# A change of banks that waits on TensorE's own semaphore instead of a drain, with a softmax round lent into the wait, and a loop that begins earlier

## The chip, the cores and the metric

One core of one Trainium2 chip. The metric is device time in microseconds of one execution. Engines are called as the profile calls them: PE (TensorE's matmuls), PEld (its weight loads), DVE (VectorE), ACT (ScalarE), POOL (GpSimd), SP (SyncE, which issues most transfers).

## The reference, cut to what matters

```python
def reference(A_x, A_wqkv, A_wo, B_x, B_w1, B_b1, B_w2, B_b2, gate_w):
    x = A_x                                   # 1 x 2048 x 576, float32
    g = sigmoid((x * gate_w).sum(-1, keepdims=True))
    a = attention(x, A_wqkv, A_wo)            # 32 heads of 18, full softmax, then @ wo
    b = gelu(layernorm(x) @ B_w1 + B_b1) @ B_w2 + B_b2     # 576 -> 4608 -> 576
    return g * a + (1 - g) * b
```

## The kernel before

Float32 operands are split into a high and a low part of TensorE's faster float32 format, and a product is the sum of three (high by high, high by low, low by high). The kernel has three stages.

The first makes q, k and v of all heads and the normalised input of the network, and stores them. The last multiplies the attention's output with wo and writes the result. Between them lies a loop of 512 steps that does the attention, and into it the network (the "mixer" of the reference) is cut in pieces. There is no scheduler: each engine runs its instructions in the order in which the Python code issues them (`tc.manual_schedule()`), and waits on semaphores for the other engines. So the order of the code is the order on TensorE.

The attention works in 32 units (a pair of heads by half of the queries), 16 steps each. What it issues:

- a *round* (`s1_round`, lines L202 and L204): two matmuls of 54 rows that make scores in two PSUM buffers, one for each head, and two maxima over them on VectorE. A unit has 32 rounds, and they run about 40 rounds ahead of the unit's exponentials, since those need each row's maximum. The PSUM pool `ps_s1` has three buffers (`NS1 = 3`), so a matmul of a round needs the buffer of the third matmul before it, and with it that one's maximum. `next_round()` issues the next round of a list of 1024.
- *scores* (`s2`, L251 and L253): two matmuls of 56 rows into one PSUM buffer (`pss`, there is one), and one exponential of 128x1024 on ScalarE that frees it.
- *values* (`pv`, L268), every other step: the probabilities of two steps by v.

The network is a Python generator (`mlp`) that yields after each *slot*, a pair of matmuls that work side by side in the array's upper and lower 64 rows. `h_pair` is an *up pair*: 27 slots of 64x512 (L489) that make two hidden tiles in two PSUM buffers, their eviction with the bias (L511 on VectorE, L512 on ScalarE), and then the gelu on ScalarE and GpSimd over the next steps. `out_pair` is an *output pair*: 24 slots of 64x288 (L614) that make 128 tokens by 576 outputs, in two PSUM banks, one for each half of the outputs. In its first 12 slots the upper rows write bank 0 and the lower rows bank 1; then they change places, so that each bank gets the sums of both. Both must not write one bank at once. So the change of banks has a wait:

```python
                elif turn == 1:
                    nc.tensor.drain()
```

(L603; 137 of the 144 output pairs. The last 7, after the last round, take other buffers instead.) At the pair's end VectorE adds both banks to the result (L593). The network is 36 groups of two up pairs and four output pairs.

`atom()` runs the generator to its next cut, and `fill(step, share)` puts one such piece at one of three places of two steps, share 0, 1 or 2. An output pair that begins in share 0 is cut after slots 7 and 15: it gets 7, 8 and 9 slots, and the change of banks, behind slot 12, lies in the piece of share 1. Two steps read so (r a round, s scores, v values): step even: r s v s r, 7 slots; step odd: r s, 8 slots with the drain behind the fifth, r s, 9 slots.

Ahead of the loop 36 rounds are done, and between the last of them pieces of up pairs stand (`between(n)`: n pieces of some 600 ns of work, each followed by `run_due`, which issues what is due on the other engines). In the loop's first steps each even step has one more round (`if step <= 2 * LEAD`, LEAD is 4).

Of the kernel before, what the change touches and what calls it, by code (L numbers as in the profile page):

```python
# [10 lines left out]
AF = mybir.ActivationFunctionType  # L11
ALU = mybir.AluOpType
# [16 lines left out]
G = 4  # L29
NFC = F // P  # L30
NG = NFC // G
ND = 288
# [7 lines left out]
LEAD = 4  # L40
# [18 lines left out]
def gated_mix_kernel(ctx: ExitStack, tc: tile.TileContext, x, wqkv, wo, w1, b1, w2, b2, gate_w, out):  # L59
    nc = tc.nc  # L60
# [101 lines left out]
    NU = 2 * NPAIR  # L162
    UNITS = [divmod(u, 2) for u in range(NU)]
    UNITS[NU - 3:NU - 1] = UNITS[NU - 2], UNITS[NU - 3]
    NR = 32
# [146 lines left out]
                defer(1, lambda: s1_finish(u))  # L312


    def mlp():
        W1, W2, HT = {}, {}, {}
        RAW = {}
# [147 lines left out]
        def h_pair(q, last, inner=False):  # L465
# [8 lines left out]
            ps = banks(q)  # L474
# [34 lines left out]
            zs = [ring2[:, 0, k, :] if q == 1 else zp.tile([P, TB], F32, name="z") for k in range(2)]  # L509
            b = [b1t[:, fc + h:fc + h + 1] for h in range(2)]  # L510
            nc.vector.tensor_scalar(zs[1], ps[1], b[1], None, op0=ALU.add)  # L511
            nc.scalar.activation(zs[0], ps[0], AF.Identity, bias=b[0])  # L512
            for h in (1, 0):
                z = zs[h]
                w = ring2[:, 1, h, :] if q == 1 else zp.tile([P, TB], F32, name="zz", bufs=3)
# [67 lines left out]
        def out_pair(i, t, acc):  # L583

            tb, g = seq[i]
            tok = slice(t * P, (t + 1) * P)
            cs = [slice(nn * ND, (nn + 1) * ND) for nn in range(2)]
            bare = not rounds

            def add(ps, base):  # L590
                for nn in range(2):
                    dst = acc[:, t, cs[nn]]
                    nc.vector.scalar_tensor_tensor(dst, ps[nn][:, :ND], 0.5, b2b[:, cs[nn]] if base else dst,  # L593
                                                   op0=ALU.mult, op1=ALU.add)
            ps = [psum(free_pool()) for _ in range(2)]
            ends = {7, 15} if piece[0] == 0 else cuts(24, (3, 2, 1)[piece[0]])
            k = 0
            for turn in range(2):
                if turn == 1 and bare:
                    add(ps, g == 0)  # L600
                    ps = [psum(free_pool()) for _ in range(2)]
                elif turn == 1:
                    nc.tensor.drain()  # L603
                for j in ORDER:
                    while (i, j) not in HT:
                        cut[0] = 3
                        yield 0
                    hh, hl = HT[i, j]
                    w_ = ready(W2, (i * (G // 2) + j // 2, j % 2))
                    for h_, p_ in ((hh, 0), (hh, 1), (hl, 0)):  # L610
                        for h in (0, 1) if turn == 0 else (1, 0):
                            r = slice(64 * h, 64 * h + 64)
                            nn = h ^ turn
                            nc.tensor.matmul(ps[nn][:, :ND], h_[r, tok], w_[p_][r, cs[nn]],  # L614
                                             start=(k == 0 or bare and k == 3 * G), stop=(k == 6 * G - 1 or bare and k == 3 * G - 1))
                        k += 1
                        if k < 6 * G:
                            if k in ends:
                                cut[0] = 1
                            yield 131  # L620
            add(ps, g == 0 and not bare)
            if g == NG - 1:
                tt = TBS[tb] * 4 + t
                nc.gpsimd.tensor_scalar(acc[:, t, :], acc[:, t, :], gate1[:, tt:tt + 1], 1.0, op0=ALU.mult, op1=ALU.mult)
                defer(12 if tb < NB - 1 else 4, lambda: nc.sync.dma_start(b_scr[tt * P:(tt + 1) * P, :], acc[:, t, :]))
            cut[0] = 2
            yield 131
# [407 lines left out]
    RING.append(ring2)  # L1035


    def out_proj():

        OT, BT, done, tmp = {}, {}, {}, {}  # L1040
# [162 lines left out]
    def between(n):  # L1203
        for part in range(n):
            t = spent[0]
            stretch(600.0)
            run_due(max(spent[0] - t, 500.0))

    while len(rounds) > NU * NR - NR - LEAD:
        between(6 if len(rounds) == NU * NR - NR else 2)  # L1210
        next_round()
        run_due(233.0)
    between(1)
    base = spent[0]
    proj = out_proj()
    over = [None]
# [29 lines left out]
    for u in range(NU):  # L1246
        for kc in range(NT):
            step = u * NT + kc
            if kc == 1:
                if u + 2 < NU:  # L1250
                    load_q(u + 2)
                if u % 2 == 0 and u // 2 + 1 < NPAIR - 1:
                    load_k(u // 2 + 1)
                    load_v(u // 2 + 1)
                elif u == NU - 5:
                    load_k(NPAIR - 1)
                elif u == NU - 4:
                    load_v(NPAIR - 1)
            at[0] = step

            next_round()
            s2(u, kc, 0)
            run_due(462.0)
            if kc % 2:
                fill(step, 1)
            elif step > 0:
                pv(step - 2)
                while ROWS:
                    ROWS.pop(0)()
                run_due(2080.0)  # L1270
                if step <= 2 * LEAD:
                    next_round()
            else:
                fill(step, 2)
            if kc % 2:
                next_round()
            s2(u, kc, 1)
            if kc % 2 == 0:

                next_round()  # L1280
            run_due(462.0)
            fill(step, 2 if kc % 2 else 0)
    pv(NSTEP - 2)
# [28 lines left out]
```

## Time and profile before

| | |
|---|---|
| median of 3 runs | 2326.66 us (2324.75 to 2327.2) |
| the profiled execution | 2327.55 us, span 2325.8 us |
| PE busy | 2295.2 us, 99% |
| DVE, ACT, POOL busy | 72%, 59%, 41% |
| drains at L603 | 137 |
| first exponential of the loop | 253.2 us from the span's start |
| last round | 2192.8 us |

Matmuls are pipelined and their ends are modelled, so a PE that is 99% busy can still be slower than it could be: what counts is the distance between the starts of matmuls. "idle before" is the engine's idle time in front of an instruction, and what stands behind the arrow is what ended it. DRAIN and waits are the sequencer's, and not counted as busy.

### The profile page before, as it was taken

Reading aid. Unit: us, or ns where it says so; the run is one execution under the profiler, and the core shown is the slowest. Engines: PE = TensorE matmul, PEld = TensorE weight load, DVE = VectorE, ACT = ScalarE, POOL = GpSimd, SP = SyncE. Lnnn points to the kernel's source line nnn. Section 1 sums busy time; section 2 is a strip of 40 time slices with the busy share of each in tenths; the row PEclk is TensorE's granted clock in tenths of the full one; section 3 lists DMA queues with packets and bytes.
Section 4 is the critical chain, followed back from the end, with each engine's and each line's share of the span. In section 5 each row is a group of like instructions: output and inputs, shape, how many; then the busy total and the mean of one; then the engine's idle time right before and its main releaser. Section 6 shows DMA issues by size and latency. Waiting matters only on the chain.

```text
span 2325.8 us, 50689 instructions
## 1 busy us (share of the span) xinstructions
PE 2295.2 (99%) x20601; PEld 1615.4 (69%) x20601; DVE 1663.7 (72%) x2921; ACT 1379.9 (59%) x1631; POOL 947.8 (41%) x936
## 2 busy tenths in 40 slices
PE   8999999999999999999999999999999999999999
PEld 7878666666666666666666666666666666666669
DVE  5675777777777777777777777777777777777545
ACT  4223666666666666666666666666666666666662
POOL 4002466566553434443444344434434443333320
PEclk9999899999999999999999999999999999999999
DMA  7756545445473524232263324233364233322346
GB/s 242 247 190 197 175 144 170 157 136 169 139 187 131 164 86 127 96 118 96 90 174 144 114 94 134 81 118 116 118 162 153 94 118 107 106 97 101 113 139 223
DMA packets 160654, 323.58 MB, mean 139 GB/s; under 512 B 56062, under 2 KB 83618, under 8 KB 149586
## 3 DMA queue, kind: packets, MB, share of 16 engines
q1 hardware_dynamic: 156582, 313.57, 43.1%
q10 hardware_dynamic: 3840, 6.78, 0.8%
q8 instruction: 162, 2.65, 0.5%
q14 instruction: 70, 0.57, 0.1%
HBM read 229.07 MB, written 95.16 MB: 139 GB/s over the span
## 4 chain that ended last, share of the span: by engine, by line
PE 90%; POOL 3%; DVE 2%; issue 2%; DMA 1%; ACT 1%; SPq 0%; ACTq 0%; POOLq 0%; DVEq 0%
PE ps L614 20%; PE ps L268 19%; PE ps L489 17%; PE pss L251 12%; PE ps L202 11%; PE ps L880 4%; PE ps L1184 3%; PE ps L898 2%; POOL zz L159 1%; POOL w L159 1%; POOL hl L159 1%; DVE m L204 1%; DMA wraw<-in_B_w_dram 1%; PE ps L795 0%; DMA p<-in_A_wqkv_dram 0%
## 5 line engine op out<-in xcount | busy, mean ns | idle before, releaser
L204 DVE TENSOR_REDUCE m<-ps 128x1 f32<-128x512 f32 x2048 | 1297.3, 684 | 431.2 <-PE ps L202 429.7
L253 ACT ACTIVATE p<-pss 128x1024 f32<-128x1024 f32 x684 | 701.7, 1026 | 456.9 <-PE pss L251 445.3
L489 PE MATMUL ps<-big,w 64*128 64x512 f32 x3834 | 514.8, 392 | 0.1
L614 PE MATMUL ps<-w,hh 64*128 64x288 f32 x4352 | 501.2, 300 | 13.8 <-ACT z L512 2.1
L159 POOL TENSOR_SCALAR zz<-zz 128x512 f32<-128x512 f32 x272 | 169.3, 622 | 827.4 <-ACT zz L575 761.8
L251 PE MATMUL pss<-qa,ka 56*128 56x512 f32 x2048 | 484.1, 437 | 3.8 <-ACT p L253 1.1
L253 ACT ACTIVATE ring<-pss 128x1024 f32<-128x1024 f32 x340 | 348.9, 1026 | 231.4 <-PE pss L251 225.6
L202 PE MATMUL ps<-ka,qa 54*128 54x512 f32 x2048 | 460.8, 410 | 2.8 <-DVE m L204 1.2
L614 PEld LDWEIGHTS ps<-w,hh 64*128 64x128 f32 x4352 | 402.4, 186 | 68.9 <-issue 42.4
L489 PEld LDWEIGHTS ps<-big,w 64*128 64x128 f32 x3834 | 390.1, 185 | 59.6 <-ACT vt L909 0.3
L159 POOL TENSOR_TENSOR zz<-zz,z 128x512 f32<-128x512 f32 x280 | 361.4, 1291 | 35.6 <-ACT zz L577 10.5
L251 PEld LDWEIGHTS pss<-qa,ka 56*128 56x128 f32 x2048 | 198.0, 185 | 254.6 <-ACT p L253 121.4
L614 PE MATMUL ps<-w,hl 64*128 64x288 f32 x2176 | 351.7, 293 | 0.0
L268 PE MATMUL ps<-p,vt 128*32 128x512 f32 x2736 | 344.5, 598 | 0.0
L202 PEld LDWEIGHTS ps<-ka,qa 54*128 54x128 f32 x2048 | 244.5, 185 | 34.0 <-DVE m L204 12.1
L614 PEld LDWEIGHTS ps<-w,hl 64*128 64x128 f32 x2176 | 236.2, 186 | 0.5
L159 POOL TENSOR_TENSOR w<-x,w 128x576 fp32r<-128x576 f32 (+1 forms) x34 | 68.3, 2012 | 308.8 <-ACT w L385 304.6
L159 POOL TENSOR_TENSOR hl<-zz,hh 128x512 fp32r<-128x512 f32 x134 | 174.1, 1300 | 19.0 <-ACT hh L538 8.1
L268 PE MATMUL ps<-ring,vt 128*32 128x512 f32 x1360 | 179.1, 598 | 0.0
L268 PEld LDWEIGHTS ps<-p,vt 128*32 128x32 f32 x2736 | 71.4, 109 | 147.3 <-issue 147.3
L593 DVE SCALAR_TENSOR_TENSOR x<-ps,x 128x288 f32<-128x288 f32 x270 | 110.8, 452 | 29.8 <-PE ps L614 16.4
L880 PE MATMUL ps<-big,wqk 128*128 128x512 f32 x504 | 123.4, 399 | 0.1
(122 smaller groups left out, 1403.3 us busy)
## 6 DMA issues: line engine op xcount, KB each, us to landing
w<-w_scr SPq DMA_DIRECT2D x54, 1152.0 KB
w<-w_scr SPq DMA_DIRECT2D x108, 576.0 KB
w_scr<-w SPq DMA_DIRECT2D x18, 1152.0 KB
w_scr<-w SPq DMA_DIRECT2D x36, 576.0 KB
qa<-qk_scr SPq DMA_DIRECT2D x192, 72.0 KB
ka<-qk_scr SPq DMA_DIRECT2D x90, 144.0 KB
x<-in_B_w_dram SPq DMA_DIRECT2D x34, 288.0 KB
qk_scr<-hh SPq DMA_DIRECT2D x36, 256.0 KB
```

The costliest lines, as they stand in the source:

```text
L159: fn(*args, **kw)
L202: nc.tensor.matmul(ps, qa[r0:r0 + 54, t * P:(t + 1) * P], ka[r0:r0 + 54, kb * TB:(kb + 1) * TB], start=True, stop=True)
L204: nc.vector.tensor_reduce(M4[u][:, h, t, kb:kb + 1], ps, axis=AX.X, op=ALU.max)
L251: nc.tensor.matmul(ps[:, h, :], ka[r0:r0 + 56, kc * P:(kc + 1) * P], qa[r0:r0 + 56, qb * TB:(qb + 1) * TB], start=True, stop=True)
L253: nc.scalar.activation(RING[n % 3][:, qb], ps, AF.Exp, scale=SCALE)
L268: nc.tensor.matmul(OB[u][r:r + 32, :], v[:, k, 19 * h:19 * h + 32], RING[c % 3][:, qb, h, :], start=(k == 0), stop=(k == NT - 1))
L489: nc.tensor.matmul(ps[h], wt[w_][r, c, :], Y[s_][r, c, :], start=(k == 0), stop=(k == 26))
L593: nc.vector.scalar_tensor_tensor(dst, ps[nn][:, :ND], 0.5, b2b[:, cs[nn]] if base else dst, op0=ALU.mult, op1=ALU.add)
L614: nc.tensor.matmul(ps[nn][:, :ND], h_[r, tok], w_[p_][r, cs[nn]], start=(k == 0 or bare and k == 3 * G), stop=(k == 6 * G - 1 or bare and ...
L880: nc.tensor.matmul(ps, w_[:, c, ms], big[:, s_, :], start=(k == 0), stop=(k == len(prods) - 1))
L898: nc.tensor.matmul(ps[:, :ND], big[:, s_, tok], w_[:, c, cs], start=(k == 0), stop=False)
L1184: nc.tensor.matmul(ps[t, n][:, :ND], OT[b][3][:, s_, tok], w_part(w_, c)[:, cs], start=(c == 0 and k == 0), stop=(c == 4 and k == 1))
```

## The change

Three things.

1. The drain goes. The last two matmuls of the first half (slot 12, upper and lower rows) each add one to a semaphore `turn`, and the first matmul of the second half waits for it. Where the change of banks lies within a piece, `lend_round()` issues the next round between the last matmul of the first half and the wait; the next `next_round()` of the loop is then left out (`loop_round()`).
2. Ahead of the loop one piece of up pairs is taken out behind round 32 (`between(6)` becomes 5), and the last piece is replaced by two rounds; the extra rounds of the loop's first steps end at step 4 instead of 8.
3. The third up pair (q = 2, the last one ahead of the loop) has both its evictions on VectorE.

```diff
+    lent = [0]
+
+    def lend_round():
+        if rounds and not lent[0]:
+            next_round()
+            lent[0] = 1
+
+    def loop_round():
+        if lent[0]:
+            lent[0] = 0
+        else:
+            next_round()
...
             nc.vector.tensor_scalar(zs[1], ps[1], b[1], None, op0=ALU.add)
-            nc.scalar.activation(zs[0], ps[0], AF.Identity, bias=b[0])
+            if q == 2:
+                nc.vector.tensor_scalar(zs[0], ps[0], b[0], None, op0=ALU.add)
+            else:
+                nc.scalar.activation(zs[0], ps[0], AF.Identity, bias=b[0])
...
                 elif turn == 1:
-                    nc.tensor.drain()
+                    if 3 * G not in ends:
+                        lend_round()
+                    turned[0] += 2
+                    nc.tensor.wait_ge(turn_sem, turned[0])
...
+                            if k == 3 * G - 1:
+                                mm.then_inc(turn_sem, 1)
+                                tc.no_tile_sem_insts.add(mm.ins.name)
+                                tc.add_to_no_dep_group(f"turn{turned[0]}", mm.ins)
+                            elif k == 3 * G and h == 0:
+                                tc.declare_fence(mm.ins, group=f"turn{turned[0] - 2}")
...
     while len(rounds) > NU * NR - NR - LEAD:
-        between(6 if len(rounds) == NU * NR - NR else 2)
+        between(5 if len(rounds) == NU * NR - NR else 2)
         next_round()
         run_due(233.0)
-    between(1)
+    for part in range(2):
+        next_round()
+        run_due(500.0)
...
-            next_round()
+            loop_round()
             s2(u, kc, 0)
...
-                if step <= 2 * LEAD:
+                if step <= LEAD:
                     next_round()
...
             if kc % 2:
-                next_round()
+                loop_round()
             s2(u, kc, 1)
             if kc % 2 == 0:
 
-                next_round()
+                loop_round()
```

What it does to the order on TensorE in the loop, at a second and third piece of an output pair. L202 is a round, L251 scores, L614 (L633 in the changed file) a slot's matmuls: six matmuls of one weight tile are three slots. "waits" names the semaphore's owner; a drain is not among these rows, and stood ahead of the first row with `w_3111,hh`. Before:

```order
L202 MATMUL ps<-ka_107,qa_105 128x512 [waits DVE_49] x2
L251 MATMUL pss<-qa_104,ka_106 128x512 [waits Activation_49]
L251 MATMUL pss<-qa_104,ka_106 128x512
L614 MATMUL ps<-w_3159,hh 128x288 x2
L614 MATMUL ps<-w_3159,hl 128x288 x2
L614 MATMUL ps<-w_3145,hh 128x288 x4
L614 MATMUL ps<-w_3145,hl 128x288 x2
L614 MATMUL ps<-w_3111,hh 128x288 x4
L614 MATMUL ps<-w_3111,hl 128x288 x2
L202 MATMUL ps<-ka_107,qa_105 128x512 [waits DVE_49] x2
L251 MATMUL pss<-qa_104,ka_106 128x512 [waits Activation_49]
L251 MATMUL pss<-qa_104,ka_106 128x512
```

The same place in the changed kernel, on the same engine:

```order
L202 MATMUL ps<-ka_107,qa_105 128x512 [waits DVE_49] x2
L251 MATMUL pss<-qa_103,ka_106 128x512 [waits Activation_49]
L251 MATMUL pss<-qa_103,ka_106 128x512
L633 MATMUL ps<-w_3111,hh 128x288 x2
L633 MATMUL ps<-w_3111,hl 128x288 x2
L633 MATMUL ps<-w_3097,hh 128x288 x4
L633 MATMUL ps<-w_3097,hl 128x288 x2
L202 MATMUL ps<-ka_107,qa_105 128x512 [waits DVE_49] x2
L633 MATMUL ps<-w_3063,hh 128x288 [waits turn]
L633 MATMUL ps<-w_3063,hh 128x288 x3
L633 MATMUL ps<-w_3063,hl 128x288 x2
L251 MATMUL pss<-qa_103,ka_106 128x512 [waits Activation_49]
```

The round that stood behind the eight slots now stands behind the first five of them, and scores follow the last three directly. All 137 waits on `turn` have a round ahead of them.

The other place is TensorE at the loop's beginning, from the transpose of the first unit's maxima (L219) on; L489 (L502 in the changed file) is an up pair's slot, `w_2206` the third up pair's weights. Before:

```order
L219 MATMUL ps<-ident,nm_2455 32x128 [waits DVE_49]
L489 MATMUL ps<-big,w_2206 128x512 x6
L202 MATMUL ps<-ka_106,qa_104 128x512 [waits DVE_49] x2
L489 MATMUL ps<-big,w_2206 128x512 x12
L202 MATMUL ps<-ka_106,qa_104 128x512 [waits Activation_49]
L202 MATMUL ps<-ka_106,qa_104 128x512 [waits DVE_49]
L489 MATMUL ps<-big,w_2206 128x512 x6
L614 MATMUL ps<-w_2051,hh 128x288 [waits Activation_49]
L614 MATMUL ps<-w_2051,hh 128x288 [waits DVE_49]
L614 MATMUL ps<-w_2051,hh 128x288 x2
```

In the changed kernel:

```order
L219 MATMUL ps<-ident,nm_2455 32x128 [waits DVE_49]
L202 MATMUL ps<-ka_106,qa_104 128x512 [waits DVE_49] x2
L502 MATMUL ps<-big,w_2206 128x512 x12
L202 MATMUL ps<-ka_106,qa_104 128x512 [waits Activation_49]
L202 MATMUL ps<-ka_106,qa_104 128x512 [waits DVE_49]
L502 MATMUL ps<-big,w_2206 128x512 x12
L202 MATMUL ps<-ka_106,qa_104 128x512 [waits DVE_49] x8
L251 MATMUL pss<-qa_103,ka_106 128x512 [waits DMAHW2_49,DMAHW1_49]
L251 MATMUL pss<-qa_103,ka_106 128x512 [waits DMAHW4_49,DMAHW3_49]
L633 MATMUL ps<-w_2051,hh 128x288 x4
```

Four rounds and the first scores now stand between the third up pair and the first output pair, which before followed each other. Later on TensorE the first up pair within the loop comes two steps earlier than before.

VectorE at the same place: L511 (L524, L526) are evictions of up pairs, L204 the rounds' maxima, L593 (L609) an output pair's addition. Before:

```order
L511 TENSOR_SCALAR ring_2268<-pss,b1t 128x512
L204 TENSOR_REDUCE m_2513<-ps 128x1 x6
L511 TENSOR_SCALAR z<-ps,b1t 128x512
L204 TENSOR_REDUCE m_2513<-ps 128x1 x10
L593 SCALAR_TENSOR_TENSOR x<-ps,b2b 128x288 x2
```

In the changed kernel:

```order
L524 TENSOR_SCALAR ring_2268<-pss,b1t 128x512
L204 TENSOR_REDUCE m_2507<-ps 128x1 x6
L524 TENSOR_SCALAR z<-ps,b1t 128x512
L526 TENSOR_SCALAR z<-ps,b1t 128x512
L204 TENSOR_REDUCE m_2507<-ps 128x1 x14
L609 SCALAR_TENSOR_TENSOR x<-ps,b2b 128x288 x2
```

Both evictions of the third up pair stand ahead of the maxima of the four rounds.

More of the change, by code (lines that the diff above doesn't have):

```diff
@@ L613, in out_pair @@
                             nn = h ^ turn
-                            nc.tensor.matmul(ps[nn][:, :ND], h_[r, tok], w_[p_][r, cs[nn]],
-                                             start=(k == 0 or bare and k == 3 * G), stop=(k == 6 * G - 1 or bare and k == 3 * G - 1))
+                            mm = nc.tensor.matmul(ps[nn][:, :ND], h_[r, tok], w_[p_][r, cs[nn]],
+                                                  start=(k == 0 or bare and k == 3 * G), stop=(k == 6 * G - 1 or bare and k == 3 * G - 1))
+                            if bare:
+                                continue
+                            if k == 3 * G - 1:
[4 more added lines that the diff above has]
+                                tc.declare_fence(mm.ins, group=f"turn{turned[0] - 2}")
                         k += 1
@@ L1035, in gated_mix_kernel @@
     RING.append(ring2)
+    turn_sem = tc.alloc_semaphore("turn")
+    turned = [0]
     def out_proj():
```

## The prediction

> **What bounds the kernel now.** I read the page's head and chain first, then one cycle of two steps on TensorE, then the same cycle on the engines that TensorE waits for.
>
> ```profile
> span 2325.8 us, 50689 instructions
> PE 2295.2 (99%) x20601; PEld 1615.4 (69%) x20601; DVE 1663.7 (72%) x2921; ACT 1379.9 (59%) x1631; POOL 947.8 (41%) x936
> PE 90%; POOL 3%; DVE 2%; issue 2%; DMA 1%; ACT 1%; SPq 0%; ACTq 0%; POOLq 0%; DVEq 0%
> ```
>
> The chain is TensorE's. Its 99% hide what the drain costs, because ends of matmuls are modelled; distances between starts tell it. A cycle with an output pair, TensorE's rows (start, us, instruction, matmuls):
>
> ```profile
> 324.95 0.40 PE L202 MATMUL ps<-ka,qa 54*128 54x512 f32 x2
> ...
> 325.59 0.43 PE L614 MATMUL ps<-w,hh 64*128 64x288 f32 x4
> 325.86 0.30 PE L614 MATMUL ps<-w,hl 64*128 64x288 f32 x2
> 325.99 0.30 PE L614 MATMUL ps<-w,hh 64*128 64x288 f32 x2
> 326.13 0.50 PE L202 MATMUL ps<-ka,qa 54*128 54x512 f32 x2
> 326.36 0.51 PE L251 MATMUL pss<-qa,ka 56*128 56x512 f32 x2
> ...
> 327.12 0.41 PE L614 MATMUL ps<-w,hl 64*128 64x288 f32 x2
> 327.61 0.53 PE L614 MATMUL ps<-w,hh 64*128 64x288 f32 x4
> 327.98 0.30 PE L614 MATMUL ps<-w,hl 64*128 64x288 f32 x2
> 328.11 0.40 PE L202 MATMUL ps<-ka,qa 54*128 54x512 f32 x2
> 328.35 0.40 PE L251 MATMUL pss<-qa,ka 56*128 56x512 f32 x2
> ...
> 330.36 1.06 PE L268 MATMUL ps<-p,vt 128*32 128x512 f32 x8
> ...
> 332.21 0.50 PE L251 MATMUL pss<-qa,ka 56*128 56x512 f32 x2
> 332.56 0.40 PE L202 MATMUL ps<-ka,qa 54*128 54x512 f32 x2
> ```
>
> A slot takes 0.13 us (325.86 to 325.99), three slots 0.40 (325.59 to 325.99), a round 0.23 (326.13 to 326.36). The slot at 327.12 is the twelfth, the last ahead of the drain. Its successor would start at 327.25 and starts at 327.61, and the three slots from there take 0.50 (to 328.11), since the first has to load its weights first. So the drain costs 0.46 us: 0.36 + 0.10. The weight loads show it as idle time that nothing visible ended, 137 times:
>
> ```profile
> 327.61 0.30 PEld L614 LDWEIGHTS ps<-w,hh 64*128 64x128 f32 x4 [0.31 <-issue]
> PEld ps L614 <- issue: 42.4, 137, 0.4
> L603 PEldq DRAIN  x137: 875/1188/1912, 256.3 to 2191.0; - x137
> ```
>
> 137 x 0.46 = 63 us are in the drains. The other place where TensorE stands still is the loop's beginning, which comes below.
>
> **The change, part by part.**
>
> *The wait in the drain's place.* It doesn't give 0.46 us back, because the second half still has to wait until the last matmuls of the first have ended, at 327.53 (327.12 + 0.41). What it brings is a round in that time. The round's matmuls take the place of the missing slot at 327.25 and stream until 327.49. A waiting load is released how soon after a matmul's end? No row shows TensorE released by its own semaphore. The nearest are VectorE behind a round, loads of scores behind an exponential, and a transpose's load behind an addition:
>
> ```profile
> 328.55 1.29 DVE L204 TENSOR_REDUCE m<-ps 128x1 f32<-128x512 f32 x2 [0.67 <-PE ps L202]
> 2232.45 1.00 ACT L253 ACTIVATE p<-pss 128x1024 f32<-128x1024 f32 x1
> 2233.50 0.51 PE L251 MATMUL pss<-qa,ka 56*128 56x512 f32 x2
> 1004.24 0.81 DVE L593 SCALAR_TENSOR_TENSOR x<-ps,x 128x288 f32<-128x288 f32 x2
> 1005.18 0.10 PEld L219 LDWEIGHTS ps<-ident,nm 128*32 128x32 f32 x1 [0.84 <-DVE x L593]
> ```
>
> That is 0.04 us (the round at 328.11 ends at 328.51), 0.05 (2233.45 to 2233.50) and 0.13 (1005.05 to 1005.18). I take 0.05, the load's own kind of row: the second half begins at 327.58, against 327.61 with the drain. Three slots at 0.50 end at 328.08, and scores follow directly, where they started at 328.35: 0.27 us sooner. But scores also wait for the exponential before them, since there is one `pss`:
>
> ```profile
> 326.97 1.03 ACT L253 ACTIVATE ring<-pss 128x1024 f32<-128x1024 f32 x1 [0.78 <-PE pss L251]
> ```
>
> It ends at 328.00, so their weights load at 328.05, and with the load's 0.10 (the scores at 2233.50 last 0.51, not 0.40) they count as started at 328.15. The gain is 0.20 us, and 137 x 0.20 = 27.4 us. Its ends: if the scores' load is covered, 137 x 0.27 = 37 us; with 0.13 for the semaphore 0.19, 26 us; and a release later than any of these rows, by 0.25 us, leaves nothing.
>
> *The round that moves.* It now follows the round before it by 1.12 us (326.13 to 327.25) instead of 1.98, and needs buffers that maxima free:
>
> ```profile
> 325.39 2.48 DVE L204 TENSOR_REDUCE m<-ps 128x1 f32<-128x512 f32 x4
> ```
>
> These are the maxima of the two rounds before it, 0.62 each. With three buffers, the second matmul of the moved round needs the third of these four, which ends at 327.25; with 0.05 to 0.13 for the release and 0.10 for the load it counts from 327.40 to 327.48 and streams to 327.71 at most, while the second half's first matmul, released at 327.58 and then loading for 0.10, cannot stream before 327.68. So VectorE costs 0.03 at most, below the exponential's bound. In this cycle VectorE was late by a copy; most are easier. Nothing else is queued differently: the nine slots, the values and the additions behind shift with TensorE, and no transfer is moved in the loop. The count of matmuls, maxima and exponentials stays.
>
> *The loop's beginning.* Rows around 249 us, TensorE, VectorE, ScalarE, and then windows with the granted clock (third figure from the end):
>
> ```profile
> 246.22 0.87 PE L489 MATMUL ps<-big,w 64*128 64x512 f32 x6
> 249.15 0.85 PE L614 MATMUL ps<-w,hh 64*128 64x288 f32 x4 [2.06 <-ACT z L512]
> 247.62 0.74 DVE L511 TENSOR_SCALAR z<-ps,b1t 128x512 f32<-128x512 f32 x1
> 245.58 0.25 ACT L221 ACTIVATE mr<-ps 32x128 fp32r<-32x128 f32 x1
> 248.43 0.67 ACT L512 ACTIVATE z<-ps,b1t 128x512 f32<-128x512 f32 x1
> 245.60:249.00 3.40, 1.49 (x12) 0.68 (x8) 2.24 (x4) 3.19 (x7) 3.25 (x4) 1.00 0.15 57
> 249.00:255.80 6.80, 5.66 (x29) 4.27 (x29) 2.77 (x5) 5.17 (x9) 5.86 (x5) 0.50 0.51 142
> 255.80:262.60 6.80, 6.72 (x43) 5.60 (x42) 3.68 (x7) 4.67 (x7) 1.28 (x1) 0.50 0.83 118
> 262.60:270.00 7.40, 7.01 (x68) 4.37 (x66) 5.80 (x11) 5.11 (x7) 4.80 (x3) 1.00 0.01 2
> 290.47 0.50 PE L202 MATMUL ps<-ka,qa 54*128 54x512 f32 x2
> 291.75 2.58 PE L489 MATMUL ps<-big,w 64*128 64x512 f32 x18
> ```
>
> The first output pair waits 2.06 us for the third up pair's eviction on ScalarE. After 3.4 us in which TensorE was busy for 1.49 the clock is granted at half, for 13.6 us. From 247.09 (end of the up pairs) to 291.75 (the next up pair) pass 44.7 us. In pieces at full clock it would be 30.8: 96 slots at 0.132 are 12.7; a cycle without its slots is 7.61 (324.95 to 332.56) - 24 x 0.132 - 0.46 = 4.0, and there are four, 16.0; 7 rounds and 2 scores beyond these at 0.23 are 2.1. So 14 us are waits and half clock.
>
> The changed order has one cycle less there; its 4.0 us come later, so 40.7 is what to compare with. Its up pairs end 0.6 us later, at 247.7, since the round behind the transpose still waits for ScalarE's row at 245.58 and now has 12 slots behind it, not 6. Then four rounds go at VectorE's pace: two evictions (2 x 0.74) from 247.8 and, behind these, a matmul with every maximum of 0.64; the eighth matmul needs the fifth maximum and comes at about 252.6. The pieces from there are 12.7 + 3 x 4.0 + 5 x 0.23 = 25.9. Waits I put at 3.9: 1.3 where two rounds and the second exponential meet, 0.8 for an addition between two output pairs that now stand side by side, 0.5 at each of two places where rounds stand on both sides of scores (290.47 to 291.75 is such a place), and 0.2 at each of four turns. That ends at 282.4, 35.3 us behind 247.09: a gain of 5.4.
>
> But the clock: between 248.5 and 250 TensorE has nothing, and then one matmul of 0.40 in each 0.64. A stretch of 3.4 us there holds 1.1 to 1.5 us of busy time, no more than the 1.49 after which the clock was halved. So I expect it halved again, for 13.6 us as before: in these 6.8 us of full-clock work get done, 2 to 3 us are waits anyway, some 4 us are lost, and of the 5.4 remain 1.3. The Trainium skill says that the clock is halved after an idle window of about 3.4 us (TensorE: Matmul & The Clock Gate, "What's actually happening"). By that page the clock stays full here, as no such stretch is wholly idle; the trace disagrees, since 2.06 us of idle time were enough.
>
> *The third pair's eviction* is in these numbers: 0.74 on VectorE ahead of the rounds, which delays their maxima by as much, and ScalarE loses 0.67 from its row of gelu work. A cost or a gain of its own it hasn't, because output banks are long free when the four rounds are through.
>
> **The sum.** Four of the 137 turns are in the beginning already: 133 x 0.20 = 26.6, and 1.3: 28 us against the profiled execution's 2327.55, which is 2325.8 of span and 1.75 around it: 2299.5. The median of the runs lies 0.9 below that execution: 2298.6.
>
> **The rivals.** *The clock stays full* at the beginning: 26.6 + 5.4 = 32 us, 2294.6. For it: no row shows where between 1.49 of 3.40 and the busy stretches the limit lies, and the four rounds spread TensorE's little work evenly. Against it: the count above. It is also what the Trainium skill's page on the clock gate, cited above, would have. *The release is slow:* if TensorE's own semaphore needs 0.25 us more than the row of scores, the turn is as long as with the drain plus the round: no gain there, 1.3 us in all, 2325.4, same. Against it: three kinds of rows between 0.04 and 0.13. *The moved round becomes the bound, and the kernel slower:* if it needs the fourth maximum and not the third, its second matmul is released at 327.87 + 0.05, counts from 328.02, streams to 328.25; three slots put the scores at 328.65 instead of 328.35, 0.30 later, and 137 x 0.30 = 41 us are lost: 2367. It decides from about 0.3 us of delay on VectorE beyond this cycle's. Against it: the pool's three buffers, and that this cycle, with VectorE running without a gap from 325.39, was already a late one.
>
> **How the numbers follow.** My forecast (gain at the turn, half clock) 0.6; full clock 0.27; slow release 0.07; moved round bound 0.03; anything between, by 0.03 more. A measurement here tells 0.2%, 4.7 us, from no change: faster 0.91, same 0.05, slower 0.04. The range runs from 0.27 at each turn (133 x 0.27 + 1.3 = 37, 2289) to 0.10 a turn, half way to the slow release, with nothing gained at the beginning (2313).
>
> **What would show it.** Right: no drain; loads of L633 behind a round released by L633's matmuls; from the round that begins an odd step (326.13) to that step's second scores (328.35) 2.0 us instead of 2.22; cycles of 7.4 instead of 7.61 us; half clock for some 13 us near 252. Wrong: long waits of L202 on L204 within the second pieces, scores waiting for exponentials by more than 0.1, or the half clock longer than before.

## The result, and the profile after

| | before | changed |
|---|---|---|
| median of the runs | 2326.65 us | 2298.43 us (2297.72 to 2301.24, 4 runs) |
| ratio, 95% interval | | 0.9881 [0.9866, 0.9896] |
| profiled execution, its span | 2327.55, 2325.8 us | 2297.90, 2296.1 us |
| drains on TensorE | 137 | 0 |

The forecast was 2298.6 in a range of 2289 to 2313. The head of the page and the chain read almost as before, as the work on TensorE is the same and it sets the end in both:

```profile
span 2296.1 us, 50544 instructions
PE 2274.7 (99%) x20601; PEld 1619.3 (71%) x20601; DVE 1656.8 (72%) x2922; ACT 1378.2 (60%) x1630; POOL 946.5 (41%) x936
...
PE 91%; POOL 3%; DVE 2%; ACT 2%; DMA 1%; issue 1%; SPq 0%; ACTq 0%; DVEq 0%; POOLq 0%
```

What changed shows in the distances between starts. A cycle with an output pair in the changed kernel, TensorE's rows (start, us, instruction, matmuls); L633 was L614, the rounds are L202, the scores L251, the values L268:

```profile
1287.88 0.40 PE L202 MATMUL ps<-ka,qa 54*128 54x512 f32 x2
...
1289.04 0.51 PE L202 MATMUL ps<-ka,qa 54*128 54x512 f32 x2
1289.27 0.51 PE L251 MATMUL pss<-qa,ka 56*128 56x512 f32 x2
...
1290.09 0.35 PE L633 MATMUL ps<-w,hl 64*128 64x288 f32 x2
1290.22 0.52 PE L202 MATMUL ps<-ka,qa 54*128 54x512 f32 x2
1290.51 0.54 PE L633 MATMUL ps<-w,hh 64*128 64x288 f32 x4
1290.87 0.31 PE L633 MATMUL ps<-w,hl 64*128 64x288 f32 x2
1291.00 0.46 PE L251 MATMUL pss<-qa,ka 56*128 56x512 f32 x2
1291.29 0.43 PE L633 MATMUL ps<-w,hh 64*128 64x288 f32 x4
...
1292.49 0.40 PE L202 MATMUL ps<-ka,qa 54*128 54x512 f32 x2
1292.73 0.41 PE L251 MATMUL pss<-qa,ka 56*128 56x512 f32 x2
1293.07 1.92 PE L268 MATMUL ps<-p,vt 128*32 128x512 f32 x16
...
1295.26 0.40 PE L202 MATMUL ps<-ka,qa 54*128 54x512 f32 x2
```

The twelfth slot starts at 1290.09 and the second half at 1290.51, 0.42 us later, hardly less than the 0.49 with the drain. But a whole round (1290.22) now stands in that time, and scores follow the second half's first three slots at once (1291.00). From the round of the odd step (1289.04) to those scores pass 1.96 us, where it was 2.22. The cycle is 1295.26 - 1287.88 = 7.38 us. Over all such cycles that can be laid on each other (113 before, 112 after) the median is 7.594 before and 7.387 after: 0.207 us less, and 137 x 0.207 = 28.4 us.

How soon TensorE's own semaphore releases it shows in the weight load of the same place:

```profile
1290.50 0.30 PEld L633 LDWEIGHTS ps<-w,hh 64*128 64x128 f32 x4
...
1290.96 0.19 PEld L251 LDWEIGHTS pss<-qa,ka 56*128 56x128 f32 x2
```

The last matmuls of the first half end at 1290.09 + 0.35 = 1290.44, and the load starts at 1290.50, 0.06 us behind. The group of these loads, all over the kernel, before and then changed (busy us, mean ns, then the idle time ahead of them and what ended it):

```profile
L614 PEld LDWEIGHTS ps<-w,hh 64*128 64x128 f32 x4352 | 402.4, 186 | 68.9 <-issue 42.4 <-ACT z L512 2.5 <-DVE x L593 1.2
L633 PEld LDWEIGHTS ps<-w,hh 64*128 64x128 f32 x4352 | 398.5, 186 | 30.3 <-DVE x L609 2.0 <-PE ps L633 1.2
```

Their idle time fell from 68.9 to 30.3 us, and its 42.4 us of "issue" are gone. Only 1.2 us of what is left, in 7 places, are put down to `PE ps L633`. The view names what ended an idle time only where that lasted over 0.15 us, and here it is 0.07 us: the load ahead of it, the round's second, ends at 1290.43.

What the scores behind the turn wait for stands on ScalarE, in the same cycle:

```profile
1288.14 1.03 ACT L253 ACTIVATE p<-pss 128x1024 f32<-128x1024 f32 x1 [1.27 <-PE pss L251]
1289.88 1.03 ACT L253 ACTIVATE p<-pss 128x1024 f32<-128x1024 f32 x1 [0.71 <-PE pss L251]
1291.56 1.02 ACT L253 ACTIVATE p<-pss 128x1024 f32<-128x1024 f32 x1 [0.65 <-PE pss L251]
1293.24 1.03 ACT L253 ACTIVATE ring<-pss 128x1024 f32<-128x1024 f32 x1 [0.66 <-PE pss L251]
```

The exponential that frees `pss` ends at 1290.91, and the load of the scores starts at 1290.96 (its row stands above, in the fence on the second half's load). So the scores, whose row says 1291.00, can't count as started before about 1291.06 (0.05 for the release, 0.10 for the load), and their successor comes 0.29 us behind them instead of 0.23. The exponentials now follow each other every 1.68 us (1289.88, 1291.56, 1293.24).

The loop's beginning, in windows of the length in which the clock changes (PEclk is third from the end):

```profile
248.96:252.37 3.41, 2.22 (x6) 0.96 (x7) 3.41 (x7) 3.01 (x6) 3.41 (x4) 1.00 0.43 130
252.37:255.79 3.42, 3.42 (x26) 3.25 (x25) 1.52 (x3) 1.03 (x1) 2.31 (x2) 0.50 0.50 140
255.79:259.20 3.41, 2.86 (x31) 2.28 (x30) 3.25 (x6) 3.36 (x5) 1.11 (x1) 1.00 1.07 174
```

The clock is halved behind the four rounds, as expected, but for 3.4 us and not for some 13. Where the two kernels have done the same work, they can be compared by place: at the transpose of a unit's maxima that starts at 436.3 us before, with rounds, scores, up pairs and 13 output pairs equal, the changed kernel is 4.0 us ahead; at the one at 2196.9, behind all 137 output pairs, 29.9; at the end 29.7.

### The profile page after: what moved, and what is told of

It reads as the page before. It is cut to its first block, busy times and chain, and to the rows that moved or that the text cites. A ratio compares the mean times of both kernels' runs of the same rounds, so it can differ in the third digit from the quotient of the medians.

```text
span 2296.1 us, 50544 instructions
## 1 busy us (share of the span) xinstructions
PE 2274.7 (99%) x20601; PEld 1619.3 (71%) x20601; DVE 1656.8 (72%) x2922; ACT 1378.2 (60%) x1630; POOL 946.5 (41%) x936
## 4 chain that ended last, share of the span: by engine, by line
PE 91%; POOL 3%; DVE 2%; ACT 2%; DMA 1%; issue 1%; SPq 0%; ACTq 0%; DVEq 0%; POOLq 0%
PE ps L268 19%; PE ps L633 19%; PE ps L502 17%; PE pss L251 13%; PE ps L202 11%; PE ps L907 4%; PE ps L1214 3%; PE ps L925 2%; POOL zz L159 1%; DVE m L204 1%; POOL w L159 1%; POOL hl L159 1%; ACT p L253 1%; PE ps L822 1%; DMA w_scr<-w 0%
## 5 line engine op out<-in xcount | busy, mean ns | idle before, releaser
L204 DVE TENSOR_REDUCE m<-ps 128x1 f32<-128x512 f32 x2048 | 1284.8, 683 | 344.6 <-PE ps L202 343.5
L502 PE MATMUL ps<-big,w 64*128 64x512 f32 x3834 | 514.6, 392 | 0.0
L633 PE MATMUL ps<-w,hh 64*128 64x288 f32 x4352 | 498.2, 297 | 1.1 <-DVE x L609 1.1
L251 PE MATMUL pss<-qa,ka 56*128 56x512 f32 x2048 | 488.0, 442 | 5.0 <-ACT p L253 2.3
L202 PE MATMUL ps<-ka,qa 54*128 54x512 f32 x2048 | 479.0, 413 | 5.1 <-DVE m L204 2.8
L502 PEld LDWEIGHTS ps<-big,w 64*128 64x128 f32 x3834 | 392.0, 185 | 57.6 <-ACT vt L936 0.3
L633 PEld LDWEIGHTS ps<-w,hh 64*128 64x128 f32 x4352 | 398.5, 186 | 30.3 <-DVE x L609 2.0
L251 PEld LDWEIGHTS pss<-qa,ka 56*128 56x128 f32 x2048 | 196.6, 184 | 259.9 <-ACT p L253 125.5
L633 PE MATMUL ps<-w,hl 64*128 64x288 f32 x2176 | 350.4, 292 | 0.0
L268 PE MATMUL ps<-p,vt 128*32 128x512 f32 x2736 | 344.6, 598 | 0.0
L202 PEld LDWEIGHTS ps<-ka,qa 54*128 54x128 f32 x2048 | 265.0, 185 | 36.5 <-DVE m L204 11.9
L633 PEld LDWEIGHTS ps<-w,hl 64*128 64x128 f32 x2176 | 235.1, 186 | 0.4
L268 PE MATMUL ps<-ring,vt 128*32 128x512 f32 x1360 | 179.1, 598 | 0.0
L268 PEld LDWEIGHTS ps<-p,vt 128*32 128x32 f32 x2736 | 71.5, 109 | 147.1 <-issue 147.1
L609 DVE SCALAR_TENSOR_TENSOR x<-ps,x 128x288 f32<-128x288 f32 x270 | 110.8, 452 | 89.1 <-PE ps L633 89.1
```

The lines of the kernel that those rows point to most:

```text
L202: nc.tensor.matmul(ps, qa[r0:r0 + 54, t * P:(t + 1) * P], ka[r0:r0 + 54, kb * TB:(kb + 1) * TB], start=True, stop=True)
L204: nc.vector.tensor_reduce(M4[u][:, h, t, kb:kb + 1], ps, axis=AX.X, op=ALU.max)
L251: nc.tensor.matmul(ps[:, h, :], ka[r0:r0 + 56, kc * P:(kc + 1) * P], qa[r0:r0 + 56, qb * TB:(qb + 1) * TB], start=True, stop=True)
L268: nc.tensor.matmul(OB[u][r:r + 32, :], v[:, k, 19 * h:19 * h + 32], RING[c % 3][:, qb, h, :], start=(k == 0), stop=(k == NT - 1))
L502: nc.tensor.matmul(ps[h], wt[w_][r, c, :], Y[s_][r, c, :], start=(k == 0), stop=(k == 26))
L633: mm = nc.tensor.matmul(ps[nn][:, :ND], h_[r, tok], w_[p_][r, cs[nn]], start=(k == 0 or bare and k == 3 * G), stop=(k == 6 * G - 1 or bare ...
```

## The experiments

The theory: the gain is the round put into the time in which TensorE has to wait for its own last matmuls. It needs both the semaphore, which doesn't wait for the round, and the round; the exponential ahead of the scores takes some of it back; the loop's beginning gives next to nothing. The rivals were that the drain itself is dear, that the round's earlier place helps by itself, and that the beginning paid a good part. Each time stands beside the kernel before on the same chip.

### The turns' change alone

The second and third part of the change are undone:

```diff
-        between(5 if len(rounds) == NU * NR - NR else 2)
+        between(6 if len(rounds) == NU * NR - NR else 2)
...
-    for part in range(2):
-        next_round()
-        run_due(500.0)
+    between(1)
...
-                if step <= LEAD:
+                if step <= 2 * LEAD:
...
-            if q == 2:
-                nc.vector.tensor_scalar(zs[0], ps[0], b[0], None, op0=ALU.add)
-            else:
-                nc.scalar.activation(zs[0], ps[0], AF.Identity, bias=b[0])
+            nc.scalar.activation(zs[0], ps[0], AF.Identity, bias=b[0])
```

> The change at the output pairs' turns alone (TensorE's own semaphore in the drain's place, the round lent ahead of it); the loop's beginning and the third pair's eviction as before. Theory (the traces compared): the cycle with an output pair is 0.207 us shorter, 137 x 0.207 = 28.4, so 27 to 29 us less than before (about 2299), and the half clock of before (13.65 us near 252) still there. Rival (the beginning gave a good part, as the clock was at half for only 3.4 us in the changed kernel): 20 us less or under, 2306 or more.

Measured: 2296.88 us against 2326.93, ratio 0.9874 [0.9861, 0.9888]: 30 us less, 1 more than the theory's bound. The cycle is 7.390 us. So the whole gain is there without the beginning, and the rival falls. The half clock was 6.8 us in this profile, not the 13.65 expected. At the place of 436.3 this profile is 4.9 us ahead of before; 13 turns of 0.204 are 2.7 of them, and the other 2.2 go with the shorter half clock, as nothing else was changed up to there.

### The beginning alone

The same edits the other way round, on the kernel before with its drain.

> The other two parts alone: the loop begins one up piece sooner, the third pair's evictions on VectorE; the drain stays. Theory: 1 to 4 us less than before (2323 to 2326), with the clock at half for 3.4 us. Rival (full gain of the rearranged beginning, the rest of the change being worth less): 5 us less or more, 2321 or under.

Measured: 2327.53 us against 2326.93, ratio 1.0003 [0.9994, 1.0012]: no difference. That misses the theory's 1 to 4 us (the interval leaves 1.4 at most), and the rival's 5 by far. By place it is level too: 1.2 us behind at 243.2, before the change begins, and 1.3 behind at 436.3. The half clock lasted 10.2 us, although TensorE's order up to the first turn is that of the changed kernel:

```profile
249.08:252.50 3.42, 1.58 (x6) 0.59 (x4) 3.42 (x6) 3.21 (x6) 3.42 (x4) 1.00 0.24 78
252.50:255.91 3.41, 3.41 (x19) 2.70 (x20) 2.71 (x5) 1.87 (x3) 3.41 (x3) 0.50 0.53 139
255.91:259.32 3.41, 3.05 (x18) 2.33 (x17) 1.94 (x4) 1.98 (x3) 0.09 (x1) 0.50 0.78 156
259.32:262.73 3.41, 3.33 (x29) 2.99 (x27) 0.54 (x1) 2.25 (x4) 1.27 (x1) 0.50 0.92 128
262.73:266.20 3.47, 3.32 (x36) 2.47 (x36) 2.02 (x4) 2.52 (x3) 0.37 (x1) 1.00 0.09 18
```

### The semaphore without the round

```diff
-                    if 3 * G not in ends:
-                        lend_round()
                     turned[0] += 2
                     nc.tensor.wait_ge(turn_sem, turned[0])
```

> The changed kernel, but no round is lent: TensorE waits on its own semaphore with nothing ahead of the wait, the round follows the piece as before. Theory (the gain is the round put into a time that has to be waited out anyway): 0.03 us at each of 137 turns, 4 us, and the beginning's 2: 2320 to 2322. Rival (the drain itself is dear and a semaphore cheap): at least half of the 28 us stays, 2311 or under.

Measured: 2325.96 us against 2326.93, ratio 0.9993 [0.9984, 1.0002]. The semaphore by itself brings no more than 4 us, and none that can be told from zero. TensorE at the turn:

```profile
1305.35 0.35 PE L631 MATMUL ps<-w,hl 64*128 64x288 f32 x2
1305.76 0.54 PE L631 MATMUL ps<-w,hh 64*128 64x288 f32 x4
1306.13 0.30 PE L631 MATMUL ps<-w,hl 64*128 64x288 f32 x2
1306.26 0.41 PE L202 MATMUL ps<-ka,qa 54*128 54x512 f32 x2
```

Nothing stands between the twelfth slot and the second half, and it starts 0.41 us later: 0.35 of the slot's own length and 0.06 of release. The median cycle is 7.573 us, 0.021 less than before, so 137 x 0.021 = 2.9 us. That the expected 2 us of the beginning aren't there agrees with the run ahead; with them missing, the theory's 2320 to 2322 was too low. The single runs lie in two groups, five from 2323.4 to 2324.3 and six from 2326.0 to 2329.3, and the profile is of the slowest. It is 1.9 us ahead of before at 2196.9, but has a second stretch of 3.4 us at half clock near 2299, 28 us ahead of its end, that no other profile shows.

### The round with the drain

```diff
                     if 3 * G not in ends:
                         lend_round()
-                    turned[0] += 2
-                    nc.tensor.wait_ge(turn_sem, turned[0])
+                    nc.tensor.drain()
```

The increments go as well; the rest is the changed kernel.

> The changed kernel with the drain kept in the semaphore's place, behind the lent round. Theory: the drain then also awaits the round's own matmuls, TensorE stands still as long as before (0.36 and 0.10 us) only one round later; nothing is gained at the turns, the beginning's 2 us stay: 2322 to 2326. Rival (the round's earlier place is what helps, since maxima and exponentials are spread better): 2310 or under.

Measured: 2336.60 us against 2326.93, ratio 1.0046 [1.0033, 1.0059]: slower by 9.7 us, where both theories had no loss.

```profile
1301.74 0.35 PE L632 MATMUL ps<-w,hl 64*128 64x288 f32 x2
1301.87 0.53 PE L202 MATMUL ps<-ka,qa 54*128 54x512 f32 x2
1302.51 0.53 PE L632 MATMUL ps<-w,hh 64*128 64x288 f32 x4
1302.88 0.30 PE L632 MATMUL ps<-w,hl 64*128 64x288 f32 x2
1303.01 0.41 PE L251 MATMUL pss<-qa,ka 56*128 56x512 f32 x2
```

Behind the round the second half starts at 1302.51, 0.64 us after the round's first matmul; I had reckoned with 0.59 (0.23 of the round and 0.36). The median cycle is 7.685 us, 0.091 longer than before (137 x 0.091 = 12.5). The missing piece is VectorE: in the median cycle the second matmul of the lent round starts 0.104 us after the first, here and in the changed kernel alike, since it waits for a maximum (in the cycle shown, the third maximum before it ends at 1301.85, and its weight load starts at 1301.90). Under the semaphore that lies in time that is waited out anyway; under the drain it is added. By place the profile is 1.6 us ahead of before at 436.3, with 3.4 us at half clock in place of 13.65, and 8.1 behind at 2196.9.

So neither half of the turn's change is worth anything alone (between -3.7 and +0.5 us, and +9.7), and both together bring 30.

### The changed kernel again, and TensorE kept busy at the beginning

The changed kernel ran once more as a base.

> The changed kernel once more, as the base beside the three other runs. Theory (how long the clock stays at half at the loop's beginning differs between executions of one kernel: 3.4, 6.8, 10.2 and 13.65 us in six profiles, in steps of 3.41): 2297 to 2300, its single runs 2 to 4 us apart.

Measured: 2299.07 us against 2326.85 (2297.64 to 2300.68), ratio 0.9880 [0.9867, 0.9894]; single runs 3.0 us apart, half clock 3.4 us, as in the first profile of this kernel. The six profiles that the theory counts are of six kernels, so this is the first pair of one kernel, and the two agree.

Beside it a kernel with matmuls that nobody reads, ahead of the fourth to eighth matmul of the four rounds:

```diff
             ps = psum(ps_s1)
+            nth = 2 * (NU * NR - NR - LEAD - len(rounds)) + h
+            if 3 <= nth < 8:
+                idle = ps_s2.tile([P, 2, TB], F32, name="pss")
+                for k in range(7 if nth == 3 else 1):
+                    nc.tensor.matmul(idle[:, 0, :], qa[:54, :P], ka[:54, :TB], start=True, stop=True)
             nc.tensor.matmul(ps, qa[r0:r0 + 54, t * P:(t + 1) * P], ...
```

> The changed kernel with eleven further matmuls where TensorE stands still at the loop's beginning: seven ahead of the fourth matmul of the four rounds, one ahead of each of the next four. They write a bank that is free there, and nobody reads it. Theory (the clock is halved after a stretch of 3.41 us in which TensorE was busy for 1.36 to 2.22 us, and VectorE sets the pace there): no half clock at the beginning, 1 to 4 us less than the changed kernel, single runs closer together. Rival 1 (the half clock costs nothing, as TensorE waits for others there anyway): no half clock, and the same time. Rival 2 (the halving doesn't come from idle time): half clock as before, same time.

```profile
247.80:251.20 3.40, 3.32 (x14) 1.97 (x12) 3.40 (x6) 3.19 (x6) 3.40 (x4) 1.00 0.20 58
251.20:254.60 3.40, 3.40 (x30) 2.52 (x28) 2.49 (x5) 1.91 (x4) 3.35 (x3) 1.00 0.54 154
254.60:258.00 3.40, 2.84 (x32) 2.35 (x33) 3.40 (x6) 3.37 (x5) 1.29 (x1) 1.00 0.84 170
```

The clock stays full. So the halving does come from the idle time, and rival 2 falls. By place it is 5.3 us ahead of before at 436.3, against 4.0 and 4.3 in the two profiles of the changed kernel: 1.0 to 1.3 us for 3.4 us at half. The time, 2297.58 us (2296.37 to 2299.44), is 1.5 below the base, which these few runs can't tell from rival 1's nothing, and the single runs lie no closer together. That the execution is ahead by place is shown; a gain in time isn't.

### The third pair's eviction back on ScalarE

The edit is the last hunk of the first experiment, on the changed kernel.

> The changed kernel with the third up pair's second eviction back on ScalarE. Theory: within 1.5 us of the changed kernel. Rival (with both evictions on VectorE the fourth matmul of the four rounds waits for two of them, 0.74 us longer than for one, and the whole beginning with it): 1 us less than the changed kernel or more.

Measured: 2297.66 us against the base's 2299.07, with single runs from 2296.70 to 2299.15. The difference, 1.4 us, lies within the spread, and both the theory's and the rival's bounds hold it. The traces show the rival's wait, in the changed kernel and then here:

```profile
249.75 3.01 PE L202 MATMUL ps<-ka,qa 54*128 54x512 f32 x5 [1.63 <-DVE m L204]
249.48 3.18 PE L202 MATMUL ps<-ka,qa 54*128 54x512 f32 x5 [0.99 <-DVE m L204]
```

The fourth matmul of the four rounds waits 0.64 us less, and the first scores come 0.65 sooner behind the up pair's last slots (5.51 us instead of 6.16). But this profile, of the slowest of the four runs, has the clock at half for 10.2 us and not for 3.4, and at the place of 436.3 it is 2.4 us ahead of before, where the changed kernel's profiles are 4.0 and 4.3. So whether the eviction on VectorE costs a microsecond in the end stays open; a gain from it is not to be seen in the times.

### Scores one slot later

```diff
-            ends = {7, 15} if piece[0] == 0 else cuts(24, (3, 2, 1)[piece[0]])
+            ends = {7, 16} if piece[0] == 0 else cuts(24, (3, 2, 1)[piece[0]])
```

This is on the turns' change alone (2296.88).

> The turns' change alone, and the pieces of an output pair cut at slots 7 and 16 instead of 7 and 15: the scores behind the turn come one slot (0.13 us) later. Theory (of the 0.27 us that the turn could give, 0.20 came, because those scores wait for the exponential before them): the scores no longer take 0.29 us but 0.23, 137 x 0.06 = 8 us less than the turns' change alone, 2289. Rival (the exponential sets the pace further on, and the next scores wait instead): 2296 to 2298.

Measured: 2308.79 us against 2326.85, ratio 0.9921 [0.9909, 0.9934]: 12 us slower than the turns' change alone, which neither theory nor rival had. TensorE, then ScalarE, in one cycle:

```profile
1289.12 0.41 PE L251 MATMUL pss<-qa,ka 56*128 56x512 f32 x2
1289.35 0.32 PE L630 MATMUL ps<-w,hh 64*128 64x288 f32 x2
...
1290.41 0.43 PE L202 MATMUL ps<-ka,qa 54*128 54x512 f32 x2
1290.71 0.50 PE L251 MATMUL pss<-qa,ka 56*128 56x512 f32 x2
1291.14 1.05 PE L268 MATMUL ps<-p,vt 128*32 128x512 f32 x6
```

```profile
1287.87 1.02 ACT L253 ACTIVATE ring<-pss 128x1024 f32<-128x1024 f32 x1 [0.71 <-PE pss L251]
1289.63 1.02 ACT L253 ACTIVATE ring<-pss 128x1024 f32<-128x1024 f32 x1 [0.74 <-PE pss L251]
1291.31 1.02 ACT L253 ACTIVATE p<-pss 128x1024 f32<-128x1024 f32 x1 [0.65 <-PE pss L251]
```

The first half of the theory holds: the scores at 1289.12 no longer wait, their successor follows in 0.23 us. But their exponential then ends at 1290.65, and the next scores at 1290.71 wait for it: the values come 0.43 behind these, where it was 0.34. The next exponential starts 1.68 us after the last one, the distance it had before. So the exponentials set the pace there, and what starts one of them later pushes the whole cycle: 7.473 us against 7.390, 137 x 0.083 = 11.4. (The half clock was 10.2 us in this profile, in place of 6.8.)

### Half the exponential

```diff
-        nc.scalar.activation(RING[n % 3][:, qb], ps, AF.Exp, scale=SCALE)
+        if kc % 2 and n >= 6:
+            nc.scalar.activation(RING[n % 3][:, qb, 0, :], ps[:, 0, :], AF.Exp, scale=SCALE)
+        else:
+            nc.scalar.activation(RING[n % 3][:, qb], ps, AF.Exp, scale=SCALE)
```

On the kernel before:

> The kernel before with part of the work left out: in odd steps from the seventh step on, the exponential takes only the first half of its scores (128x512 in place of 128x1024), the other half keeps older values. It is the base for the next run. Theory: the cycle with an output pair stays within 0.02 us of 7.59, since TensorE waits for the drain there and not for the exponential. Rival (the second scores of the odd step and those of the even step already follow each other at the exponential's pace, 1.66 us): 0.05 us less or more per cycle.

And on the changed kernel:

> The changed kernel with the same work left out. Theory (the turn gives 0.207 us and not 0.27 because the scores behind it wait for the exponential ahead of them): the scores last 0.23 us and not 0.29, the cycle is 0.26 to 0.27 us shorter than the one of the kernel before with the same half exponentials, and the time 35 to 38 us less than that kernel's. Rival (the rest of the 0.27 is lost elsewhere in the turn): 0.20 to 0.21 us per cycle, 27 to 30 us.

Measured: 2305.48 and 2270.91 us, against 2326.91 for the kernel before. The base's median cycle with an output pair is 7.584 us, within 0.02 of 7.594 as the theory said; its 21 us come mostly from the cycles with up pairs: the 88 that have nothing else of the network take 786.4 us before and 771.2 here, 15 us less. The changed kernel with half exponentials is 34.6 us below its base, and its median cycle is 7.324: 0.260 less, not 0.207. The scores behind the turn, TensorE:

```profile
1206.52 0.59 PE L202 MATMUL ps<-ka,qa 54*128 54x512 f32 x2
1206.85 0.52 PE L636 MATMUL ps<-w,hh 64*128 64x288 f32 x4
1207.22 0.29 PE L636 MATMUL ps<-w,hl 64*128 64x288 f32 x2
1207.35 0.40 PE L251 MATMUL pss<-qa,ka 56*128 56x512 f32 x2
1207.59 0.43 PE L636 MATMUL ps<-w,hh 64*128 64x288 f32 x4
```

They last 0.40 and not 0.46, and the next slot follows in 0.24. The time falls just below the 35 expected, but far from the rival's 30. That the exponential takes back 0.05 to 0.06 us per turn is shown.

### The turns' change with a busy beginning

Eight matmuls ahead of the first output pair, three and five ahead of the first two scores, into the values' bank:

```diff
+    def warm(n, qa, ka):
+        idle = psum(ps_o)
+        for k in range(n):
+            nc.tensor.matmul(idle, qa[:54, :P], ka[:54, :TB], start=True, stop=True)
...
+        if n == 0:
+            warm(5 if qb else 3, qa, ka)
...
+            if i == 0 and t == 0:
+                warm(8, QA[0], KA[0])
```

> The turns' change alone, with matmuls that nobody reads where TensorE stands still at that kernel's beginning: eight ahead of the first output pair, three and five ahead of the first two scores, into the bank of the values, which is free until then. Theory (half clock there costs 0.3 us for each us that it lasts; 6.8 us in the profile of the turns' change alone): no half clock near 250, 1 to 3 us less than the turns' change alone, about 2295, and by that the fastest of all. Rival (no halving, but those matmuls delay the pairs behind them): 2297 or more.

Measured: 2296.84 us against 2326.91, ratio 0.9871 [0.9856, 0.9886]. The clock stayed full, and by place it is 5.8 us ahead of before at 436.3 (the turns' change alone: 4.9). In time it can't be told from the turns' change alone, 2296.88: the theory's 2295 isn't reached, and the rival's 2297 or more can't be told from it either. These two are the fastest versions: 30.1 us less than before each, where the changed kernel has 28.2 and 27.8. Those 2 us are less than the single runs of one kernel lie apart.

## Why the prediction was right, point by point

- *The wait.* The release was put at 0.05 us from a row of scores behind an exponential; it is 0.06. The second half starts 0.42 us after the twelfth slot (predicted: 0.46). That the semaphore alone is worth 0.03 a turn came out as 0.021, and as nothing in the time. The rival of a slow release is out.
- *The gain of a turn.* Predicted 0.20, measured 0.207; 137 x 0.207 = 28.4 of the profile's 29.7 us. The bound by the exponential was the right one: with half exponentials the turn gives 0.260, where the prediction had 0.27 without that bound.
- *The moved round.* VectorE was to cost 0.03 at most. Its wait is longer than that, 0.10 between the round's two matmuls, but it is hidden: the second half starts when the release allows. The run with the drain shows the price where it isn't hidden. The rival that this round becomes the bound is out.
- *The loop's beginning: the mis-sized step.* Half clock of 13.6 us at a cost of 4 was wrong in length: 3.4 us, at a cost of 1.0 to 1.3. The gain of 5.4 ahead of it was too large as well. The first up pair within the loop came at 284.2, and at 282.8 with the clock kept full, where 282.4 was predicted; but up to 436.3 some of that is lost again. Without the half clock 5.3 - 9 x 0.207 = 3.4 us are left there for the beginning and its four turns, and in the changed kernel 4.0 - 1.9 = 2.1, where the sum had 1.3. And it isn't the new order that brings them: the turns' change alone is 4.9 ahead at the same place. That two errors of opposite sign met made this term look right. That the whole forecast lies 0.2 us from the median is luck too, as the single runs lie 3.5 us apart.
- *The third pair's eviction.* No gain in the times, as said. The delay that it brings the four rounds is there, 0.65 us at the first scores; a cost of up to 1.4 us isn't excluded.
- *The clock as a rival (2294.6).* The Trainium skill's rule of an idle window of about 3.4 us (TensorE: Matmul & The Clock Gate, "What's actually happening") would have kept the clock full. The trace disagrees: windows with 1.58 and, by modelled ends, 2.22 us of busy time were followed by half clock. Filled windows kept it full, and that agrees with the page.
- *What would show it.* No drain, 1.96 us for the predicted 2.0, a cycle of 7.39 for 7.4: right. Loads released by L633's matmuls: right in the starts; the view names the releaser in 7 places only, as the others are too short for it. Half clock of 13 us: wrong.

## What to carry to other kernels

A wait that has to be waited out is worth what independent work can be put into it: here neither the cheaper wait nor the moved work paid alone, and a drain behind the moved work waits for that work too. Before moving such work, follow the next single-buffered hand-over behind it (here scores and exponential), because it sets how much of the gap comes back: moving the scores 0.13 us later there cost 0.083 us a turn. When a gain is put together from one term repeated 137 times and one that happens once, test the single one alone; here it was worth nothing.

## What the runs showed of the hardware

- The time at half clock is a multiple of 3.41 us, and one order of work gives different ones: 13.65 us in the kernel before, and 6.8 in its form with half exponentials, which is the same program up to there. With the changed beginning it was 3.4 in four profiles with the lent round, 10.2 in the two without it, and 10.2 too with the lent round and the third pair's eviction on ScalarE. With the old beginning and the lent round it was 6.8 and 10.2, in two kernels that differ in where the output pairs are cut. The halving begins 238.9 or 242.3 us behind the first record of the clock, 70 or 71 times 3.413. So where the idle time falls on that grid may decide how long it lasts; that wasn't tried by itself. The Trainium skill (TensorE: Matmul & The Clock Gate, "What's actually happening") tells of a window of 3413 ns that runs freely, so that a change of clock falls differently from run to run: the rows agree, with steps of 3.413 us. It lets one busy window bring the clock back. In the fence on the beginning alone, a window that was busy throughout by modelled ends (252.50 to 255.91) was followed by two more at half.
- Half clock at a place where TensorE waits for others part of the time cost 0.3 to 0.4 us for each us that it lasted in one comparison (1.0 to 1.3 for 3.4, the changed kernel with and without further matmuls), and less in the other (0.9 for 6.8, the turns' change alone with and without them). What the further matmuls themselves cost is in both.
- The drain is hardly dearer than the wait on TensorE's own semaphore. From the modelled end of the last matmul to the next start it took 0.08 us (327.53 to 327.61), the semaphore 0.07 (1290.44 to 1290.51). What a drain can't do is to leave out the work behind the one awaited.
